# A Strassen form for the products of attention into the model, with the outputs normalized by a row from DRAM

## The chip, the cores and the metric

The kernel runs on one core of one Trainium2 chip. The metric is the device time of one execution in microseconds (us), the median of the runs shown. Five engines work side by side, each in the order of its own program: TensorE (PE) multiplies matrices, VectorE (DVE), ScalarE (ACT) and GpSimd (POOL) work on rows of 128 partitions, and SyncE (SP) issues transfers between DRAM and the memory on the chip. TensorE writes to PSUM, which has eight banks of 128 x 512 single-precision numbers, and the other engines read the result from there.

## The reference, cut to what matters

The sizes are S = 2048 rows, D = 576, 32 query heads on 16 key heads of width 128, the last W = 512 keys only, and a hidden width F = 4608, all in single precision.

```python
sa, ca, ga, sb, cb, gb = split(silu(c) @ w_mod)          # six rows of D
h = layernorm(x) * (1 + ca) + sa
q = (h @ wq) by heads;  k, v = caches[:, :, Sk - W:, :]  # two query heads per key head
o = softmax(q k^T / sqrt(128)) v
x = x + ga * (o @ wo)
h = layernorm(x) * (1 + cb) + sb
out = x + gb * ((silu(h @ w1) * (h @ w3)) @ w2)
```

The change is in `o @ wo`. Head by head this is a sum over 32 products of a [2048, 128] matrix with a [128, 576] one.

## The kernel before, in words

The rows are four blocks of 512. The first half of attention works on blocks 0 and 1, the second on blocks 2 and 3. A *slot* is one head on one block; `slots` lists 128 of them, 64 for each half, and slots 4k to 4k + 3 are two heads (2k' and 2k' + 1) on the two blocks. A slot is cut into four *steps* of 128 rows. A single-precision product is made from three fast ones: each operand is split into a high part, rounded to fp32r by a cast on ACT, and a low part, the difference, and high x high, high x low and low x high are added in PSUM. `split` (L82) does it: ACT casts, and DVE or POOL subtracts.

In iteration i of the main loop (at the end of the function) each step t transposes a quarter of the probabilities of slot i - 1 (`turn`), makes the scores of slot i, a quarter of the query of slot i + 1, and `attend_out(i - 2, t)`. After the fourth step `values(i - 1)` multiplies the probabilities into the values and leaves them in the PSUM tile `po`.

`values` (L344) splits `po` into a high and a low part, ACT casting and DVE subtracting, and takes the reciprocal r of the softmax's sums. `attend_out` (L361) calls `back` (L276), six matmuls 128x288 into the single PSUM tile E, of two banks, and DVE evicts E with one instruction, accumulator + r * E (L366). So the division by the softmax's sum is made when the product is evicted, row by row.

Everything that is not in those steps is listed by hand: `at(i, t, task)` puts a task behind step t of iteration i, and `run(i, t)` issues the tasks of a step in the order in which they were listed. All engines and SP's queue keep the program's order. Transfers wait in SP's queue for what they need, and the ones behind them wait too.

Such tasks are: the loads and splits of the query weights (`load_in`, `split_in`, POOL subtracting), of the output weights (`load_out`, a gate multiplication on POOL, `split_out`), of keys and values; and the making of the weights for the second part of the kernel, the gated MLP. That part multiplies pairs of blocks by Strassen's seven block products already. Its weights are prepared during attention: `load_raw` issues twelve transfers of a block of w1 and w3, `make_set` in seven steps makes seven sums, splits them (ACT casts, POOL subtracts) and stores each to DRAM (L499). `load_rows` loads two row blocks of w2, `make_rows` multiplies them by the gate and takes four differences on POOL in one step (its step -1), and then in seven steps splits and stores the seven operands (`keep`, L536). `load_oset` loads them back. There are 36 gate sets and 19 pairs of rows, so 55 items of seven steps.

In the second half the first two blocks, whose attention is complete, are also normalized and turned for the MLP (`norm`, `store_h`), and `combine` with `stage` makes the seven sums of h and stores them to DRAM: 21 steps on ACT, POOL and SP. `load_set` loads them. Buffers come from rings by tag: `hs` has 7 large buffers for h, raw weights and sets; `xn`, `w`, `hf`, `raw`, `o` are smaller ones.

Of the kernel before, what the change touches and what calls it, by code (L numbers as in the profile page):

```python
# [16 lines left out]
P = 128  # L17
# [21 lines left out]
def tile_block(  # L39
# [112 lines left out]

    norms = {}

    def norm_stats(b, t):
# [138 lines left out]
    n = len(slots)  # L294
    state = [dict() for _ in range(n)]
    hT, wqs, keys, vals, wos = {}, {}, {}, {}, {}
# [47 lines left out]
    def values(i):  # L344
        half, h, b = slots[i]
        st = state[i]
        vh, vl = vals[half, h // 2]
        pt = st["pt"]
        po = bank("A", "po")
        for j in range(KC):  # L350
            nc.tensor.matmul(po, vh[:, j, :], pt[0][:, j, :], start=j == 0, stop=False)  # L351
            nc.tensor.matmul(po, vl[:, j, :], pt[0][:, j, :], start=False, stop=False)  # L352
            nc.tensor.matmul(po, vh[:, j, :], pt[1][:, j, :], start=False, stop=j == KC - 1)  # L353
        oh = pool.tile([P, SB], F32R, tag="ah", name="oth", bufs=3)
        ol = pool.tile([P, SB], F32R, tag="al", name="otl", bufs=3)
        split(oh, ol, po, nc.vector)
        r = odd.tile([P, ST], F32, tag="r", name="r", bufs=3)
        nc.vector.reciprocal(r, st["l"])
        st["o"], st["r"] = (oh, ol), r

    def attend_out(i, t):  # L361
        half, h, b = slots[i]
        st = state[i]
        back(st["o"], wos[half, h], t)
        a = half_split(acc[b][:, t, :])
        nc.vector.scalar_tensor_tensor(a, E[:, :, :HALF], st["r"][:, t : t + 1], a, op0=ALU.mult, op1=ALU.add)  # L366
# [26 lines left out]
    def combine_tiles(pair):  # L393

        if pair == 0:
            a = pool.tile([P, DC + 1, SB], F32, tag="hs", name="hc", bufs=HB)
            return [a[:, k, :] for k in range(DC + 1)]
        tiles = [pool.tile([P, SB], F32, tag="xn", name="hc", bufs=ST) for _ in range(4)]
        return tiles + [pool.tile([P, SB], F32, tag="raw", name="hc", bufs=RB)]
# [33 lines left out]
    def combine(pair, c, step, tiles):  # L433
# [6 lines left out]
        elif step == 1:  # L440
            sub(h12, h12, h11)
            stage(pair, "p2", c, h21)
        elif step == 2:
            sub(h11, h22, h12)
            stage(pair, "p7", c, t3)
        elif step == 3:
            stage(pair, "p5", c, h12)
        elif step == 4:
            stage(pair, "p6", c, h11)
            sub(h21, h21, h11)  # L450
        elif step == 5:
            stage(pair, "p3", c, h22)
        else:
            stage(pair, "p4", c, h21)

    def load_set(pair, k):
# [5 lines left out]
    works = {}  # L462
    staged = [0]

    def staging(shape, name):

        staged[0] += 1
        tag, bufs = (("xn", ST), ("w", 8))[staged[0] % 2]
        return pool.tile(shape, F32R, tag=tag, name=name, bufs=bufs)
# [45 lines left out]
    odram[LAST, 4] = dram.tile([P, 2, 2, HALF], F32, name="od_plain")  # L515

    def chunks(d):

        return d if d < G else FLIP if d == G else d - G - 1

    def load_rows(p):

        whole = pool.tile([P, 7, HALF], F32, tag="hs", name="w2raw", bufs=HB)
        for j in range(2):
            f = NF - 1 - j if p == FLIP else 2 * p + j
            nc.sync.dma_start(whole[:, 2 * j : 2 * j + 2, :], half_split(w2[f * P : (f + 1) * P, :]))
        works["o", p] = whole
# [10 lines left out]
    def make_rows(p, n):  # L538
# [3 lines left out]
        if n < 0:  # L542
            for j in range(2):
                r = whole[:, 2 * j : 2 * j + 2, :]
                nc.gpsimd.tensor_mul(r, r, half_split(gates["b"]))
            nc.gpsimd.tensor_sub(t1, b12, b11)
# [48 lines left out]
    def finish(pair, t, eng):  # L595

        m15, m6 = msums[pair][0][t], msums[pair][1][t // 2][:, t % 2, :]
        a = half_split(acc[2 * pair + 1][:, t, :])
        eng.tensor_add(m6, m6, m15[:, 0, :])
# [3 lines left out]
        eng.tensor_add(m15[:, 1, :], m15[:, 1, :], m6)  # L603
        if pair == 0:
            store_out(1, t)

# [15 lines left out]
    def down(d, u):  # L622
# [23 lines left out]
        else:  # L646
            nc.vector.tensor_add(into, ps[:, :, :HALF], into)

    def multiply(ps, jobs):
# [128 lines left out]
    def gate(into, key, kind):  # L778
        nc.gpsimd.tensor_mul(into[key], into[key], gates[kind])

    first = {}
    for i, (half, h, b) in enumerate(slots):
        first.setdefault((half, h), i)
    for key, i in first.items():
        h, kv = key[1], (key[0], key[1] // 2)
        if i >= 2:
            at(i - 3, 1, load, wqs, key, load_in, wq, h * DH)
            at(i - 2, 1, put, wqs, key, split_in)
        at(*(i - 2, 1) if i > 2 else (0, -1), load, wos, key, load_out, wo, h * DH)
        at(*(i - 1, 0) if i > 2 else (1, 1), gate, wos, key, "a")  # L790
        at(max(i - 1, 1), 2, put, wos, key, split_out)
        if i and h % 2 == 0:
# [6 lines left out]
    last_group = len(groups) - 1  # L799
    early = [4 * i + t for lo, hi in ((10, 57), (66, 75)) for i in range(lo, hi) for t in range(ST)]  # L800
    late = [4 * i + t for i in range(85, 117) for t in range(ST)]
    items = []
    for p in range(G + 1):
        for f in (2 * p, 2 * p + 1) if p < G else ():
            items += [(load_raw, make_set, f, k) for k in range(7)]
        items += [(load_rows, make_rows, p, k) for k in range(7)]
    soon = len(early) * 5 // 4
    for number, (loader, maker, w, k) in enumerate(items):
        if number < soon:
            step = early[number * len(early) // soon]  # L810
        else:
            step = late[(number - soon) * len(late) // (len(items) - soon)]
        if k == 0:
            lead = 6 if maker is make_set else 11
            at((step - lead) // 4, (step - lead) % 4, loader, w)
            if maker is make_rows:
                at((step - 4) // 4, (step - 4) % 4, maker, w, -1)
        at(step // 4, step % 4, maker, w, k)
    for k, (i, t) in zip(ORDER, ((n - 4, 0), (n - 4, 1), (n - 4, 3), (n - 3, 0), (n - 3, 1), (n - 3, 2), (n - 2, 0))):
# [15 lines left out]
    for d in range(2 * G):  # L835
# [7 lines left out]
        for q, (i, t) in times:  # L843
            at(("m", i), t, load_oset, d, q)
    for pair, i in ((0, 2 * HQ + 23), (1, ("m", 14))):
        at(i, 0, split_x, pair)
# [23 lines left out]

    for i, b in ((52, 2), (2 * HQ + 6, 0)):
        for k in range(2):
# [19 lines left out]

    for b, i in ((0, 2 * HQ + 12), (1, 2 * HQ + 16)):
        norm(i, b)
        for m in range(DC + 1):
            at(i + 1 + m // 3, m % 3, store_h, b, m, "T", "hf")
    at(2 * HQ + 21, -1, begin_parts, 0)
# [94 lines left out]
    for i in range(n + 2):  # L992
        run(i, -1)
        for t in range(ST):
# [11 lines left out]
            if 2 <= i:  # L1006
                attend_out(i - 2, t)
            run(i, t)
# [32 lines left out]
```

## Time and profile before

| what | value |
| --- | --- |
| median of 3 runs | 3064.2 us (3063.02 to 3065.59) |
| the profiled execution, its own time | 3066.29 us |
| its span, first to last instruction | 3064.5 us |
| mean granted clock of TensorE | 0.996 |
| bytes moved by DMA | 523.13 MB, mean 171 GB/s |
| a slot in the second half | 13.9 us |

In the profile, PE is TensorE's matmuls and PEld its weight loads; L282 is line 282 of the kernel; `pe<-o,oth` names what an instruction writes and what it reads. Matmuls overlap, so the length of one record is longer than the time after which the next one starts. A row of the grouped view has the busy time, the mean of one in ns, and the idle time ahead of it with what ended it. A row of the timeline has the start, the length, the engine and the line.

### The profile page before, as it was taken

The numbers are of one execution on the slowest core, as the hardware profiler recorded it, in microseconds if no ns is written. First come the engines' busy times: TensorE is split into PE (matmuls) and PEld (weight loads), VectorE is DVE, ScalarE is ACT, GpSimd is POOL, SyncE is SP. The second block draws the span as 40 slices with busy tenths as digits, with TensorE's granted clock in tenths as the row PEclk, the third lists the DMA queues.
The fourth block names the chain that finished last, engine by engine and source line by source line (L and its number), as shares of the span: only waits on it lengthen the run. The fifth ranks groups of instructions, "written<-read, shape, count | busy, mean of one in ns | idle before, by whom it ended". The sixth has DMA issues, their size and how long they took to land.

```text
span 3064.5 us, 47936 instructions
## 1 busy us (share of the span) xinstructions
PE 3027.4 (99%) x16948; PEld 2654.4 (87%) x16948; DVE 2002.5 (65%) x3042; ACT 1481.7 (48%) x3107; POOL 1635.3 (53%) x1656
## 2 busy tenths in 40 slices
PE   7999999999999999999999999999999999999998
PEld 6888888888888888888888888888888888888887
DVE  6776676777777777777777766555555555555555
ACT  4556666666666665666665553333333222322222
POOL 3257887888734731667775103346555463443444
PEclk8999999999999999999999999999999999999999
DMA  4235546555512532354544135667666766666664
GB/s 143 76 130 191 184 163 198 182 184 184 179 42 76 181 101 65 127 183 168 160 163 149 40 141 187 210 219 259 240 229 219 279 238 193 203 200 203 199 197 141
DMA packets 330128, 523.13 MB, mean 171 GB/s; under 512 B 32800, under 2 KB 161824, under 8 KB 328096
## 3 DMA queue, kind: packets, MB, share of 16 engines
q1 hardware_dynamic: 329280, 520.06, 51.5%
q8 instruction: 135, 2.21, 0.3%
q14 instruction: 105, 0.86, 0.1%
q10 hardware_dynamic: 608, 0.00, 0.0%
HBM read 369.76 MB, written 150.18 MB: 170 GB/s over the span
## 4 chain that ended last, share of the span: by engine, by line
PE 94%; DVE 2%; POOL 2%; ACT 1%; issue 1%; DMA 1%; SPq 0%; ACTq 0%; POOLq 0%; DVEq 0%
PE py L577 15%; PE pe L282 13%; PE px L577 11%; PE pq L266 11%; PE pt L335 7%; PE pf L653 6%; PE pe L653 6%; PE po L353 4%; PE po L352 4%; PE po L351 4%; PE pss L317 4%; PE pss L315 4%; PE pss L316 4%; PE pq L274 2%; PE pt L252 0%
## 5 line engine op out<-in xcount | busy, mean ns | idle before, releaser
L325 ACT ACTIVATE p<-pss,nm 128x512 f32<-128x512 f32 x512 | 353.3, 690 | 367.4 <-DVE nm L319 367.1
L577 PE MATMUL py<-hset,wset 128*128 128x512 f32 x2016 | 506.9, 391 | 0.0
L366 DVE SCALAR_TENSOR_TENSOR acc<-pe,r,acc 128x576 f32<-128x576 f32 x512 | 416.8, 814 | 53.6 <-PE pe L282 47.9
L319 DVE TENSOR_REDUCE nm<-pss 128x1 f32<-128x512 f32 x512 | 349.7, 683 | 118.2 <-PE pss L317 118.0
L577 PEld LDWEIGHTS py<-hset,wset 128*128 128x128 f32 x2016 | 362.6, 188 | 58.9
L577 PE MATMUL px<-hset,wset 128*128 128x512 f32 x1512 | 380.1, 391 | 0.0
L282 PEld LDWEIGHTS pe<-o,oth 128*128 128x128 f32 x2048 | 326.7, 188 | 48.7 <-DVE acc L366 6.1
L342 DVE TENSOR_TENSOR ptl<-pt,pth 128x512 fp32r<-128x512 f32 x512 | 349.0, 682 | 16.1 <-ACT pth L336 15.6
L282 PE MATMUL pe<-o,oth 128*128 128x288 f32 x2048 | 355.8, 296 | 2.7 <-DVE acc L366 2.6
L336 ACT CAST pth<-pt 128x512 fp32r<-128x512 f32 x512 | 301.1, 588 | 37.1 <-PE pt L335 33.3
L577 PEld LDWEIGHTS px<-hset,wset 128*128 128x128 f32 x1512 | 275.6, 188 | 49.4
L335 PE MATMUL pt<-ident,p 128*128 128x128 f32 x2048 | 307.7, 273 | 4.6 <-DVE ptl L342 2.6
L85 POOL TENSOR_TENSOR akv<-u,akv 128x512 fp32r<-128x512 f32 x141 | 182.1, 1302 | 237.8 <-ACT akv L84 236.3
L335 PEld LDWEIGHTS pt<-ident,p 128*128 128x128 f32 x2048 | 249.8, 141 | 18.6 <-issue 3.0
L315 PE MATMUL pss<-kh,qh 128*128 128x512 f32 x512 | 244.9, 478 | 0.7 <-ACT qh L84 0.7
L85 DVE TENSOR_TENSOR otl<-po,oth 128x512 fp32r<-128x512 f32 x128 | 88.6, 692 | 225.8 <-ACT oth L84 225.8
L497 POOL TENSOR_TENSOR wmade<-wraw,wmade 128x256 fp32r<-128x256 f32 x252 | 186.6, 740 | 80.5 <-ACT wmade L496 62.0
L282 PE MATMUL pe<-o,otl 128*128 128x288 f32 x1024 | 219.0, 295 | 0.0
L84 ACT CAST oth<-po 128x512 fp32r<-128x512 f32 x128 | 75.1, 587 | 295.6 <-PE po L353 295.6
L317 PE MATMUL pss<-kh,ql 128*128 128x512 f32 x512 | 202.9, 396 | 0.0
L316 PE MATMUL pss<-kl,qh 128*128 128x512 f32 x512 | 202.6, 396 | 0.0
L353 PE MATMUL po<-ptl,vh 128*128 128x512 f32 x512 | 201.1, 393 | 1.2 <-DVE ptl L342 1.2
(181 smaller groups left out, 6522.7 us busy)
## 6 DMA issues: line engine op xcount, KB each, us to landing
oset<-od SPq DMA_DIRECT2D x106, 576.0 KB, 4.8
od<-omade SPq DMA_DIRECT2D x133, 288.0 KB, 2.7
oraw<-in_A_wo SPq DMA_DIRECT2D x64, 288.0 KB, 3.1
wraw<-in_B_w SPq DMA_DIRECT2D x144, 128.0 KB, 2.7
wraw<-in_A_wq SPq DMA_DIRECT2D x64, 256.0 KB, 3.2
w2raw<-in_B_w SPq DMA_DIRECT2D x38, 288.0 KB, 3.6
oset<-od SPq DMA_DIRECT2D x35, 288.0 KB, 3.3
wraw<-in_B_w SPq DMA_DIRECT2D x288, 32.0 KB, 2.1
```

The source lines that it names most:

```text
L266: nc.tensor.matmul(ps, (wh if k < 2 else wl)[:, m, :], hT[DC + m if k == 1 else m], start=s == 0, stop=False,)
L282: nc.tensor.matmul(E[:, h, :HALF], a[:, rows], b[:, h * HALF : (h + 1) * HALF], start=n == 0, stop=n == 2)
L315: nc.tensor.matmul(pss, st["qh"][:, rows], kh, start=True, stop=False)
L316: nc.tensor.matmul(pss, st["qh"][:, rows], kl, start=False, stop=False)
L317: nc.tensor.matmul(pss, st["ql"][:, rows], kh, start=False, stop=True)
L319: nc.vector.tensor_reduce(nm, pss, axis=AX.X, op=ALU.max, negate=True)
L325: nc.scalar.activation(p, pss, AF.Exp, bias=nm, accum_out=st["l"][:, t : t + 1])
L335: nc.tensor.transpose(ps[:, j, :], p[:, j * P : (j + 1) * P], ident)
L342: nc.vector.tensor_sub(pt[1][:, :, cols], state[i]["t"], pt[0][:, :, cols].bitcast(F32))
L366: nc.vector.scalar_tensor_tensor(a, E[:, :, :HALF], st["r"][:, t : t + 1], a, op0=ALU.mult, op1=ALU.add)
L577: nc.tensor.matmul(ps, w[:, a, :], h[:, b, :], start=start and n == 0, stop=stop and n == 6, skip_group_check=True)
L653: nc.tensor.matmul(ps[:, h, :HALF], a[:, rows], w[:, b, :], start=m == 0, stop=m == 2)
```

## The change

For heads 4 to 27 of the second half (slots 72 to 119, twelve groups of two heads on two blocks, `FAST`), the products into the model are made as seven block products. With X the 2 x 2 blocks of outputs (two blocks of rows, two heads) and B the 2 x 2 blocks of the output weights (two heads, two halves of D), Winograd's form of Strassen's method needs seven products of sums of X and of B in place of eight. A group has 84 matmuls 128x288 in place of 96.

The sums need outputs that are already divided by the softmax's sums, and in `po` the rows of the model lie along the free dimension. So `invert` writes the reciprocals of a slot to DRAM, transposed, and `spread` reads them back as one row over all 128 partitions; `values` multiplies `po` by it. The weights of these heads are made like those of w2, as twelve more pairs of rows among the items, loaded with `load_oset`. `out_sum` makes the sums of X on POOL, `out_split` splits the seven operands (two with POOL, five with DVE), and `out_unit` makes 14 units of six matmuls into E, each with one addition on DVE. They run from the third step of the fifth slot after a group's first slot on, one unit in a step, with two steps left out in each sixteen.

The partial sums lie where the accumulators of blocks 0 and 1 were: these are stored to DRAM ahead and loaded back after attention, and the subtraction that readies block 1 for the MLP moves to the MLP's second group. Block 3's accumulator is kept as a difference while the new form runs, so heads 28 and 29 use weights that are also split as a difference (`put_turned`); `finish_out` and `finish_out_first` add the sums up. The items' steps are spread anew: 33 of them in slots 10 to 56 as before, and the other 22 with the twelve new ones in slots 66 to 116 (before, the rest lay in slots 66 to 74 and 85 to 116). The statistics, the normalization and the combining of blocks 0 and 1 move ahead, and the combining is made in 15 slots where it had 24.

```diff
+    FAST = range(18, 30)
 def values(i):
...
+        if i // 4 in FAST:
+            nc.vector.tensor_mul(blocks[i], po, sums_home[3])
+            return
...
+    def invert(i):
+        r = odd.tile([P, ST], F32, tag="r", name="r", bufs=3)
+        nc.vector.reciprocal(r, state[i]["l"])
+        state[i]["row"] = dram.tile([ST, P], F32, name=f"r{i}")
+        nc.sync.dma_start(state[i]["row"].rearrange("t p -> p t"), r)
+
+    def spread(i):
+        row = state[i].pop("row").rearrange("t p -> (t p)")
+        nc.sync.dma_start(sums_home[3], row.partition_broadcast(P))
...
+    PAIRS_OF_HEADS = [("a", k - 16) for k in FAST]
...
+            w, f = (wo, 2 * p[1] + j) if type(p) is tuple else (w2, NF - 1 - j if p == FLIP else 2 * p + j)
...
+    def out_unit(k, u):
+        b, d = slots[4 * k][0], ("a", k - 16)
+        m15, m6 = sums_home[:2]
+        if u < 4:
+            q, into, jobs = 0, half_split(acc[b + 1][:, u, :]), [("p4", 0, u), ("p7", 1, u)]
...
+        multiply(E, [(halves[d, name], osets[d, q][:, i], r) for name, i, r in jobs])
+        if k == FAST[0] and q in (1, 2):
+            nc.vector.tensor_copy(into, E[:, :, :HALF])
+        else:
+            nc.vector.tensor_add(into, E[:, :, :HALF], into)
+
+    def out_sum(k, what):
+        x00, x01, x10, x11 = (blocks[4 * k + i] for i in range(4))
+        if what == "s3":
+            nc.gpsimd.tensor_sub(sums_home[2], x00, x01)
+        elif what == "s1":
+            nc.gpsimd.tensor_add(x01, x01, x11)
+        elif what == "s2":
+            nc.gpsimd.tensor_sub(x11, x01, x00)
+        else:
+            nc.gpsimd.tensor_sub(x10, x10, x11)
+
+    def out_split(k, name):
...
+        hi, lo = [pool.tile([P, SB], F32R, tag=t, name=f"o{t}", bufs=3) for t in ("ah", "al")]
+        split(hi, lo, x, nc.gpsimd if name in ("p7", "p2") else nc.vector)
+        halves[("a", k - 16), name] = hi, lo
...
+    EARLY = 33
+    late, places = made[EARLY:], []
+    for j, p in enumerate(PAIRS_OF_HEADS):
+        lo, hi = (len(late) * k // len(PAIRS_OF_HEADS) for k in (j, j + 1))
+        places += [(load_rows, make_rows, p), *late[lo:hi]]
+    for these, lo, hi in ((made[:EARLY], 10, 57), (places, 66, 117)):
+        for number, (loader, maker, w) in enumerate(these):
+            for k in range(7):
+                step = 4 * lo + (7 * number + k) * 4 * (hi - lo) // (7 * len(these))
+                if k == 0:
+                    lead = 6 if maker is make_set else 7
+                    at((step - lead) // 4, (step - lead) % 4, loader, w)
+                    if maker is make_rows:
+                        at((step - 4) // 4, (step - 4) % 4, maker, w, -1)
+                at(step // 4, step % 4, maker, w, k)
...
-        i = 2 * HQ + 22 + 8 * c
+        i = 2 * HQ + 18 + 5 * c
         at(i, -1, fill_parts, 0, c)
         for step in range(7):
-            at(i + 1 + step, 1, combine_parts, 0, c, step)
+            at(i + 1 + step // 2, 1 + 2 * (step % 2), combine_parts, 0, c, step)
...
+    for k in FAST:
+        s, d = 4 * k, ("a", k - 16)
+        for i in range(s, s + 4):
+            at(i + 1, 0, invert, i)
+            at(i + 1, 2, spread, i)
+        for what, i, t in (("s3", 3, 1), ("s1", 5, 0), ("s2", 5, 2), ("s4", 7, 2)):
+            at(s + i, t, out_sum, k, what)
+        for name, i, t in (("p7", 4, 1), ("p4", 5, 0), ("p6", 5, 3), ("p1", 6, 1), ("p5", 6, 2), ("p2", 7, 1), ("p3", 8, 0)):
+            at(s + i, t, out_split, k, name)
+        for q, (i, t) in enumerate(((4, 3), (5, 2), (6, 0), (7, 0))):
+            at(s + i, t, load_oset, d, q)
+        for u in range(14):
+            step = 4 * (s + 5) + 2 + u + (u >= 10)
+            at(step // 4, step % 4 + 0.5, out_unit, k, u)
...
-                attend_out(i - 2, t)
+                if (i - 2) // 4 not in FAST:
+                    attend_out(i - 2, t)
+            run(i, t + 0.5)
             run(i, t)
```

More of the change, by code (lines that the diff above doesn't have):

```diff
@@ L363, in attend_out @@
         st = state[i]
-        back(st["o"], wos[half, h], t)
+        back(st["o"], wos.get((half, h, b)) or wos[half, h], t)
         a = half_split(acc[b][:, t, :])
@@ L844, in tile_block @@
             at(("m", i), t, load_oset, d, q)
-    for pair, i in ((0, 2 * HQ + 23), (1, ("m", 14))):
+    for pair, i in ((0, ("m", 1)), (1, ("m", 14))):
         at(i, 0, split_x, pair)
```

116 lines of the change are left out of this document (78 added, 38 removed).

## The prediction, made before the changed kernel was run

> **What bounds the kernel now.** I read the page first: busy shares, then the chain that ended last.
>
> ```profile
> PE 3027.4 (99%) x16948; PEld 2654.4 (87%) x16948; DVE 2002.5 (65%) x3042; ACT 1481.7 (48%) x3107; POOL 1635.3 (53%) x1656
> ...
> PE 94%; DVE 2%; POOL 2%; ACT 1%; issue 1%; DMA 1%; SPq 0%; ACTq 0%; POOLq 0%; DVEq 0%
> ```
>
> TensorE sets the end: 94% of the chain. A matmul taken away is a gain only while DVE, ScalarE, GpSimd (POOL) and SyncE's queue (SP) keep up. So the second view is busy time by stretch (window, length, then PE, PEld, DVE, ACT, POOL, and last clock, DMA share, GB/s):
>
> ```profile
> 0.00:100.00 100.00, 81.20 (x411) 66.78 (x412) 70.67 (x119) 49.95 (x96) 34.29 (x36) 0.90 0.42 129
> 300.00:700.00 400.00, 399.18 (x2278) 349.58 (x2277) 283.76 (x440) 259.12 (x592) 321.05 (x390) 1.00 0.56 183
> 1000.00:1300.00 300.00, 299.41 (x1726) 262.94 (x1725) 218.42 (x362) 179.70 (x396) 148.36 (x165) 1.00 0.37 120
> 1300.00:1500.00 200.00, 200.00 (x1145) 175.76 (x1144) 141.19 (x220) 126.08 (x286) 143.39 (x158) 1.00 0.53 176
> ```
>
> PE is full in both halves of attention, even where POOL is 80% busy (300 to 700). In the second half POOL has only 49 to 72%.
>
> Third, the time of one slot (one head on one block), from the first and last of the 30 reciprocals between two answers on L358: (1849.5 - 1431.9)/30 = 13.92 us.
>
> ```profile
> L358 DVE RECIPROCAL r<-l x98: 166/168/170, 64.3 to 1431.9; 128x4 f32<-128x4 f32 x98
> L358 DVE RECIPROCAL r<-l x128: 166/168/170, 64.3 to 1849.5; 128x4 f32<-128x4 f32 x128
> ```
>
> Fourth, the order of time inside one slot (start, length, engine):
>
> ```profile
> 500.41 0.70 PE L282 MATMUL pe<-o,oth 128*128 128x288 f32 x4
> 500.94 0.43 PE L282 MATMUL pe<-o,otl 128*128 128x288 f32 x2
> 501.21 0.60 PE L335 MATMUL pt<-ident,p 128*128 128x128 f32 x4
> 501.42 0.82 DVE L366 SCALAR_TENSOR_TENSOR acc<-pe,r,acc 128x576 f32<-128x576 f32 x1 [0.21 <-PE pe L282]
> ...
> 506.80 0.40 PE L353 MATMUL po<-ptl,vh 128*128 128x512 f32 x1
> 507.04 0.60 PE L335 MATMUL pt<-ident,p 128*128 128x128 f32 x4
> ...
> 509.39 0.43 PE L282 MATMUL pe<-o,otl 128*128 128x288 f32 x2
> 509.65 0.60 PE L335 MATMUL pt<-ident,p 128*128 128x128 f32 x4
> ...
> 511.48 0.69 PE L282 MATMUL pe<-o,oth 128*128 128x288 f32 x4
> ```
>
> A step (a quarter of a slot) is 507.04 to 509.65, 2.61 us; the last has more query products and the values behind it. The products into the model are issued every (500.94 - 500.41)/4 = 0.133 us. That pitch, not the 0.3 us of a single record, is what one of them is worth.
>
> **The products.** Four slots (two heads, two blocks) took 4 x 24 = 96 such matmuls; seven block products take 7 x 12 = 84. Twelve groups: 144 fewer, 144 x 0.133 = **-19.1 us**.
>
> **The end of the new stretch.** Units are issued five slots behind their group, the plain product two. So in slots 122 to 125 twelve steps hold both, back to back in the one PSUM tile E. The second waits for the first's eviction: L366 above ends at 502.24 where the next matmul began at 501.21, 1.03 us. Twelve times: **+12.4 us**. (The 14 steps without E at the start are in the 19.1 already.)
>
> **DVE and ScalarE.** Per group DVE loses 16 evictions of 0.814 and gains 14 additions of 0.752 and five splits from SBUF at 1.153; the multiplication by the row has the size of the subtraction it replaces (0.692).
>
> ```profile
> L366 DVE SCALAR_TENSOR_TENSOR acc<-pe,r,acc 128x576 f32<-128x576 f32 x512 | 416.8, 814 | 53.6 <-PE pe L282 47.9
> L647 DVE TENSOR_TENSOR acc<-pe,acc 128x576 f32<-128x576 f32 x140 | 105.3, 752 | 53.9 <-PE pe L653 52.8
> L85 DVE TENSOR_TENSOR otl<-po,oth 128x512 fp32r<-128x512 f32 x128 | 88.6, 692 | 225.8 <-ACT oth L84 225.8
> L85 DVE TENSOR_TENSOR aal<-u,aah 128x512 fp32r<-128x512 f32 x37 | 42.7, 1153 | 26.0 <-ACT aah L84 26.0
> ```
>
> That is -13.0 + 10.5 + 5.8 = +3.3 us, 0.8 per slot on 218/300 = 73% of 13.9, so 11 of 13.5 us: counted at nothing behind TensorE (without that cover 48 x 0.8 = 38 us). ScalarE is at 60 to 63% and stays below. The moved accumulators, the later subtraction for the first pair and the smaller pool of staging tiles I put at nothing: other heads' products hide them.
>
> **The row, which is the term that decides.** It must pass through SP. At the slot's first step the reciprocal is written to DRAM, at its third the row is read back over all partitions, and DVE's multiplication behind the values waits for it. Queued behind that wait are DVE's next maximum, low part and eviction of E; PE's next unit waits for the latter. How late may the row be? From the third step's end (501.21) to the end of the values (507.20) are 6.0 us. If the multiplication starts there, 0.69 + 0.69 + 0.68 + 0.75 us later E is free, at 510.0, and PE wants it at 511.48: with hand-overs some 1.2 us more. So the row must land 7.2 us after the third step. A 256 KB load lands in 3.1 us, 3.2 with the fuller queue, so SP may come to it **4.0 us** late.
>
> ```profile
> oset<-od SPq DMA_DIRECT2D x106, 576.0 KB, 4.8
> ...
> kvraw<-in_A_v_cache SPq DMA_DIRECT2D x32, 256.0 KB, 3.1
> hd0p<-hst SPq DMA_DIRECT2D x35, 256.0 KB, 2.3
> ```
>
> (Fuller, because a group adds four loads of products' weights, 2.0 MB, seven stores of 288 KB and four rows of 256 KB: 5 MB in 54 us, 93 GB/s on the 120 to 176 of the windows. At 4.8 us, as the larger loads take, each late row would cost 1.6 more.)
>
> The write is 512 elements of 4 bytes; the nearest is the load of c by single elements (4.0/4.3/4.6 us, the last line below), 4.3.
>
> ```profile
> 1400.29 0.98 SPq L478 DMA_DIRECT2D wraw<-in_B_w  x2
> ...
> 1404.30 1.88 SPq L481 DMA_DIRECT2D wraw<-in_B_w  x4
> ...
> 1430.36 10.44 SPq L499 DMA_DIRECT2D wd31p<-wmade  x2
> ...
> DMA to landing us min/median/max: 4.0/4.3/4.6
> ```
>
> SP goes in program order. The first two rows are the first and the last of the twelve issues of one gate set's load: 5.9 us. The third shows SP held 10.4 us by stores whose POOL work was late; nobody needed soon what lay behind them. Why POOL was late:
>
> ```profile
> 1421.27 0.46 POOL L498 TENSOR_TENSOR wmade<-wraw,wmade 64x128 fp32r<-64x128 f32 x1
> 1422.95 1.57 POOL L85 TENSOR_TENSOR wl<-wraw,wh 128x640 fp32r<-128x640 f32 x1 [1.23 <-ACT wh L84]
> ...
> 1430.41 2.83 POOL L545 TENSOR_TENSOR w2raw<-w2raw,gate_b 128x576 f32<-128x576 f32 x2
> 1433.20 0.81 POOL L546 TENSOR_TENSOR w2raw<-w2raw 128x288 f32<-128x288 f32 x1
> ...
> 1437.91 1.30 POOL L85 TENSOR_TENSOR vl<-kvraw,vh 128x512 fp32r<-128x512 f32 x1
> ...
> 1419.61 0.81 DVE L366 SCALAR_TENSOR_TENSOR acc<-pe,r,acc 128x576 f32<-128x576 f32 x1
> 1433.26 0.82 DVE L366 SCALAR_TENSOR_TENSOR acc<-pe,r,acc 128x576 f32<-128x576 f32 x1
> ```
>
> The gate and four differences of one pair of rows are 2.83 + 4 x 0.81 = 6.1 us in one step. The two DVE rows mark the ends of first steps: POOL finished those steps' work 2.1 (1421.73) and 5.9 us (1439.21) late. So b, the lag with which SP reaches a step, is 2.1 to 5.9; I take 3, nearer the lower, which had no burst ahead of it.
>
> The new list puts 34 items in slots 66 to 117, item n beginning at step 264 + 6n. Loads of gate sets stand at 258 + 6n, bursts of rows at 260 + 6n: always a first or third step, where the row's two issues stand behind them. From slot 73 there are twelve set loads. Eight stand in third steps, where the read is 5.9 + b - 4.0 = 1.9 + b too late; four in first steps, where write and landing (5.9 + 0.4 + 4.3 = 10.6) overrun the two steps between (5.2) by 5.4, so 1.4 + b. With b = 3: 8 x 4.9 + 4 x 4.4 = **57 us**. Six bursts stand in first steps: POOL has 6.1 and two steps' makes (some 3.3) to do within 5.2, so 0.2 + b: **19 us**. In third steps a burst comes behind the read and is mostly drained: nothing.
>
> ```profile
> L497 POOL TENSOR_TENSOR wmade<-wraw,wmade 128x256 fp32r<-128x256 f32 x252 | 186.6, 740 | 80.5 <-ACT wmade L496 62.0 <-issue 7.1 <-POOL wmade L498 4.2
> L498 POOL TENSOR_TENSOR wmade<-wraw,wmade 64x128 fp32r<-64x128 f32 x252 | 116.2, 461 | 19.8
> L533 POOL TENSOR_TENSOR omade<-w2raw,omade 128x288 fp32r<-128x288 f32 x134 | 106.8, 810 | 79.9 <-ACT omade L532 65.3 <-DMA wraw<-in_B_w 6.6 <-DMA hc<-h 5.2
> L693 POOL TENSOR_TENSOR s<-u,u 128x512 f32<-128x512 f32 x35 | 45.3, 1294 | 65.0 <-DVE u L750 65.0
> L490 POOL TENSOR_TENSOR wraw<-wraw 128x384 f32<-128x384 f32 x36 | 36.6, 1017 | 1.0
> ```
>
> In slots 82 to 97 the combining of h is now pressed into 15 slots. An item is 7 x 1.20 + 4 x 1.02 = 12.5 us (set) or 2 x 1.42 + 11 x 0.81 = 11.8 (rows); 10.7 of them are 130 us. Four groups' sums and splits are 24 x 1.29 = 31, query weights and values 8 x 1.57 + 4 x 1.30 = 18, combining 12 x 1.29 + 28 x 1.3 = 52. POOL: 231 us. PE: 16 x (13.92 - 0.40) = 216. POOL overflows by 15 us and never gets its lag down: between 15 us more and 5.9 (the larger b) in each of the 12 slots that combine, 71. I take **40**, about the middle, since no row is nearer to either.
>
> The sum: -19.1 + 12.4 + 57 + 19 + 40 = **+109 us** on the profiled execution's 3066.3 (span 3064.5), which is 2.1 above the median: 3175 there, **3174** as a median. With b = 2.1 and 15 for the combining it is +68, with landings of 2.3 instead of 3.2 us at 31 late rows another -28: 3104. With b = 5.9 and 71: +192, 3256.
>
> The Trainium skill's page "DMA: Bandwidth & Descriptors", section "Anatomy of one DMA", gives a fixed 2.0 us plus bytes/436 GB/s: 2.6 us for the row and 2.0 for the write. By that estimate the third-step delays shrink by 0.6 us each, and the sum by some 20 us. The loads of this trace took 3.1, so the sum keeps the rows.
>
> **Rivals.** *The row comes in time*: SP's lag costs nothing, as it does now, because the loads run ahead in the pauses that POOL still has (it is 80% busy at 300 to 700 with PE full). Then -19.1 + 12.4 = -7, 3057, and 3045 if the double steps hide too. For it: DVE no longer waits 1.8 us per slot for ScalarE (225.8/128). Against it: the 10.4 us row. It turns where SP's lag at the third step stays under 4.0 us.
>
> *Only POOL's work counts*: it overflows in slots 82 to 97 but each row comes early enough: -7 + 15 = +8, 3072. Against it: the row is needed in the slot in which it is made.
>
> *The clock falls too.* In the first 100 us PE idled 18.8 and was granted 0.90, so 10 us lost for 18.8 idle, 0.53 per us. The 116 us of stalls would cost 62 more: 3236. The Trainium skill's "TensorE: Matmul & The Clock Gate", Part 1, says that an idle window brings the clock back to half; that row agrees, though start-up may be the reason, and no row shows it for a stall.
>
> **How the numbers follow.** Likeliest 0.60; row in time 0.22; only POOL 0.10; clock 0.08. The likeliest's own range is 3104 to 3256. Both signs hold weight, so the range goes to 3055, which takes in half of the first rival, and ends at 3240. A change under about 0.2% (6 us) can't be told from none. Faster takes 0.14 from the first rival, the rest of it, 0.08, is no change; slower 0.78.
>
> **What would show it.** DVE's multiplication in slots 72 to 119 idle behind a DMA of the row, over 1 us, most in slots 82 to 98; PE under 95% there; SP's store of a made set holding the row's issues; idle PE in slots 122 to 125 behind L366, about 1 us each. If DVE waits for TensorE instead and PE stays at 99%, the row's term is wrong; if POOL's lag stays under 4 us in slots 82 to 97, so is the 40.

## The result

The changed kernel takes **3497.9 us** (median of 4 runs, 3496.8 to 3500.9) against 3064.9: a ratio of 1.142, 95% interval 1.140 to 1.143. It is slower, as forecast, but by 433 us where 109 were forecast, and outside the range.

The page of the changed kernel: busy shares, the clock by slices, and the chain that ended last.

```profile
PE 3119.4 (89%) x16804; PEld 2703.7 (77%) x16804; DVE 2024.4 (58%) x3082; ACT 1511.9 (43%) x3205; POOL 1830.2 (52%) x1861
...
PEclk9999999999998888787887889999999999999999
...
PE 40%; DMA 15%; DVE 4%; POOL 4%; issue 4%; ACT 2%; SPq 1%; DVEq 0%; POOLq 0%; ACTq 0%
PE py L603 13%; PE px L603 9%; DMA r<-r 7%; PE pe L718 7%; PE pf L718 6%; DMA acc<-r 5%; PE pt L339 1%; DMA wraw<-in_A_wq 1%; PE pq L267 1%; DVE nm L323 1%; DVE os L360 1%; PE pe L283 1%; POOL omade L559 1%; DVE oal L85 1%; SPq L500 0%
```

TensorE's share of the chain falls from 94 to 40%. Two transfers stand in it, the reciprocals' write (`r<-r`) and the row's read (`acc<-r`). By stretch (columns as in the prediction):

```profile
300.00:700.00 400.00, 397.97 (x2271) 348.67 (x2270) 282.05 (x437) 256.88 (x587) 316.11 (x383) 1.00 0.55 181
1100.00:1500.00 400.00, 270.56 (x1310) 225.61 (x1310) 171.02 (x272) 163.67 (x375) 229.28 (x251) 0.83 0.65 152
1500.00:2100.00 600.00, 419.46 (x2028) 354.63 (x2027) 273.40 (x432) 237.75 (x549) 302.46 (x321) 0.84 0.63 139
```

The first half is untouched. In the new stretch TensorE is busy 68 to 70% at a clock of 0.83 to 0.84, and nothing else is full: neither DVE (43 to 46%) nor POOL (50 to 57%). Something is waited for in turn. The instructions on L360 (the multiplication by the row), their idle time, and the landings of the two transfers, first the write and then the read:

```profile
L360 DVE TENSOR_TENSOR os<-po,acc x48: 691/692/693, 1092.5 to 2138.1; 128x512 f32<-128x512 f32 x48
...
  DMA acc<-r: 370.2, 46
...
DMA to landing us min/median/max: 9.2/9.5/11.0
...
DMA to landing us min/median/max: 5.3/5.6/6.1
```

Of 48 multiplications 46 waited for the row, 370 us together, and 47 intervals took 1045.6 us: **22.2 us a slot** where it was 13.9. The chain of waits over two slots, in order of time:

```profile
1506.96 0.69 DVE os L360
1507.65 0.61 DVE nm L323
...
1512.21 9.58 DMA r<-r
1521.79 0.02 issue
1521.81 5.62 DMA acc<-r
...
1527.55 0.69 DVE os L360
1528.24 0.61 DVE nm L323
...
1530.86 1.31 DVE oal L85
1532.16 0.10 DVE r L374
1532.26 0.02 issue
1532.28 11.00 DMA r<-r
1543.28 0.02 issue
1543.30 6.07 DMA acc<-r
```

A reader should see a ring here: write, read, multiplication, a few DVE and POOL instructions, the next slot's reciprocal, the next write. Averaged over the slots, by the starts in the timeline, a turn is 11.7 us from the issue of the write to that of the read, 4.9 from there to the multiplication, 3.3 to the next reciprocal and 2.5 to the next write; the last part, and what the first has over the landing of 9.5, is mostly SP coming late. The whole loss lies in attention: its last reciprocal, at 1849.5 us before, now comes at

```profile
L368 DVE RECIPROCAL r<-l x80: 166/168/172, 63.3 to 2281.4; 128x4 f32<-128x4 f32 x80
```

which is 432 us later, and from there to the end of the span are 1215 us in both.

### The profile page after: what moved, and what is told of

Read it like the earlier page. It is cut to its first block, busy times and chain, and to the rows that moved or that the text cites. A ratio compares the mean times of both kernels' runs of the same rounds, so it can differ in the third digit from the quotient of the medians.

```text
span 3496.4 us, 48599 instructions
## 1 busy us (share of the span) xinstructions
PE 3119.4 (89%) x16804; PEld 2703.7 (77%) x16804; DVE 2024.4 (58%) x3082; ACT 1511.9 (43%) x3205; POOL 1830.2 (52%) x1861
## 4 chain that ended last, share of the span: by engine, by line
PE 40%; DMA 15%; DVE 4%; POOL 4%; issue 4%; ACT 2%; SPq 1%; DVEq 0%; POOLq 0%; ACTq 0%
PE py L603 13%; PE px L603 9%; DMA r<-r 7%; PE pe L718 7%; PE pf L718 6%; DMA acc<-r 5%; PE pt L339 1%; DMA wraw<-in_A_wq 1%; PE pq L267 1%; DVE nm L323 1%; DVE os L360 1%; PE pe L283 1%; POOL omade L559 1%; DVE oal L85 1%; SPq L500 0%
## 5 line engine op out<-in xcount | busy, mean ns | idle before, releaser
L339 PE MATMUL pt<-ident,p 128*128 128x128 f32 x2048 | 329.6, 286 | 169.6 <-DVE kl L257 73.5
L339 PEld LDWEIGHTS pt<-ident,p 128*128 128x128 f32 x2048 | 263.0, 148 | 195.5 <-issue 98.3
L559 POOL TENSOR_TENSOR omade<-w2raw,omade 128x288 fp32r<-128x288 f32 x218 | 175.7, 817 | 264.6 <-ACT omade L558 248.9
L718 PE MATMUL pe<-oset,oah 128*128 128x288 f32 x672 | 160.3, 329 | 150.5 <-ACT oah L84 85.9
L388 DVE SCALAR_TENSOR_TENSOR acc<-pe,r,acc 128x576 f32<-128x576 f32 x320 | 260.4, 814 | 33.3 <-PE pe L283 29.5
L718 PEld LDWEIGHTS pe<-oset,oah 128*128 128x128 f32 x672 | 130.4, 214 | 177.6 <-ACT oah L84 88.5
L319 PE MATMUL pss<-kh,qh 128*128 128x512 f32 x512 | 257.4, 503 | 0.7 <-ACT qh L84 0.7
L360 DVE TENSOR_TENSOR os<-po,acc 128x512 f32<-128x512 f32 x48 | 33.2, 692 | 384.3 <-DMA acc<-r 370.2
L283 PEld LDWEIGHTS pe<-o,oth 128*128 128x128 f32 x1216 | 194.1, 188 | 31.1 <-DVE acc L388 6.1
L283 PE MATMUL pe<-o,oth 128*128 128x288 f32 x1216 | 212.1, 296 | 2.4 <-DVE acc L388 2.2
```

Source lines behind the costliest of these rows:

```text
L283: nc.tensor.matmul(E[:, h, :HALF], a[:, rows], b[:, h * HALF : (h + 1) * HALF], start=n == 0, stop=n == 2)
L319: nc.tensor.matmul(pss, st["qh"][:, rows], kh, start=True, stop=False)
L339: nc.tensor.transpose(ps[:, j, :], p[:, j * P : (j + 1) * P], ident)
L718: nc.tensor.matmul(ps[:, h, :HALF], a[:, rows], w[:, b, :], start=m == 0, stop=m == 2)
```

## The experiments

Times are of single runs beside a kernel before of 3064 to 3068, with four runs where an interval is given; the four of `const_row` lie between 3192 and 3198, so a few microseconds between single runs say nothing. Line numbers are those of each kernel.

| run | time, us | from one multiplication to the next, us |
| --- | --- | --- |
| the change | 3498 | 22.2 |
| `early`: write listed earlier | 3436 | 20.7 |
| `no_items_row`: no later items, row as changed | 3370 | 19.7 |
| `runs16`: write in runs of 16 bytes | 3349 | 19.1 |
| `no_write`: read only | 3327 | 18.7 |
| `no_items_early`: no later items, write earlier | 3238 | 16.8 |
| `pitch8`: row of ones, slow combining | 3200 | 16.1 |
| `row_on_act`: row through ScalarE's queue | 3198 | 16.1 |
| `const_row`: row of ones | 3197 | 16.0 |
| `relief`: that, early weights, slow combining, three sums on DVE, exact | 3193 | 16.0 |
| `fewer_issues`: row of ones, loads in 6 pieces | 3193 | 15.9 |
| `best1`: row through ScalarE's queue, early weights, sums on DVE, exact | 3189 | 15.7 |
| `oset_early`: row of ones, early weights | 3175 | 15.6 |
| `xdve`: row of ones, early weights, sums on DVE | 3172 | 15.4 |
| `no_items`: row of ones, no later items | 3094 | 13.9 |
| `no_items_order`: the same, other order in double steps | 3088 | 13.9 |

**How much is the row?** A row of ones takes both transfers away.

```diff
+        nc.gpsimd.memset(sums_home[3], 1.0)
...
-            at(i + 1, 0, invert, i)
-            at(i + 1, 2, spread, i)
```

> The changed kernel without both transfers of the row: DVE multiplies the outputs of heads 4 to 27 by a row of ones that stays in place, so these heads are not divided by their softmax sums; all else is the change. Theory A (the two landings of the row, 9.5 and 5.6 us one behind the other, are nearly the whole loss): DVE's multiplication waits for the values alone and the time falls to 3058 to 3080 us. Theory B (POOL's overflow in slots 82 to 97 and SP's lag hold TensorE by themselves): 3100 us or more, with PE under 95% in those slots. The product term of the prediction (-19.1 + 12.4) would show as 3057 if nothing else is lost.

Measured: 3196.7 us, ratio 1.043 (1.041 to 1.045). That is theory B's range, but both theories hold a part: the row costs 301 us, and 132 stay without it. TensorE's waits in the new stretch of this run:

```profile
PE pe L718 <- DMA oset<-ad: 41.9, 8, 11.9
PE pt L339 <- DVE kl L257: 12.7, 4, 5.5
PE pe L718 <- DVE acc L388: 10.6, 9, 1.8
```

The longest is for the loads of the products' weights, which stand in SP's queue as the row did. The sum of the prediction did not have them.

**Read, write, or order?** Three runs change one thing each.

```diff
# no_write: no reciprocal, every read is of one fixed row of ones
-        nc.sync.dma_start(sums_home[3], row.partition_broadcast(P))
+        nc.sync.dma_start(sums_home[3], sums_home[4].partition_broadcast(P))
...
-            at(i + 1, 0, invert, i)
...
# runs16; the multiplication then reads the row at a stride of four
...
-        state[i]["row"] = dram.tile([ST, P], F32, name=f"r{i}")
-        nc.sync.dma_start(state[i]["row"].rearrange("t p -> p t"), r)
+        state[i]["row"] = dram.tile([P, ST], F32, name=f"r{i}")
+        nc.sync.dma_start(state[i]["row"], r)
...
# early
-            at(i + 1, 0, invert, i)
+            at(i, 3, invert, i)
```

> The row is read from DRAM for every slot as in the change, but from one fixed row of ones; no reciprocal is taken and none written (heads 4 to 27 are not divided by their softmax sums). Theory A: without the write's 9.5 us the read of 5.6 us still lands 5.6 us after SP comes to it, against 7.2 allowed, so SP may be 1.6 us late: I expect 60 to 160 us of loss to stay (3120 to 3220 us). Theory C (the write is what costs, the read is hidden): under 3090 us. Theory B: hardly below 3400.

> The same result by another layout in DRAM: each partition writes its four reciprocals as one run of 16 bytes, 128 runs in place of 512 single elements; the row then holds them in the order row, step, and DVE reads it with a stride of four. Nothing else is changed. If the 9.5 us are the number of pieces, the write lands in 3.5 to 5 us, each slot is some 5 us shorter where DVE waited, and the time is 3200 to 3300 us. If they are the distance to DRAM, the write stays over 8 us and the time within 40 us of 3498.

> The write of single elements is kept, but reciprocal and write are listed behind the last step of the slot itself, ahead of the multiplication of the slot before, and no longer behind the first step of the next; the read stays where it was. Theory A: the write begins about 5.4 us earlier and no longer waits for the multiplication before it, so an undisturbed slot has its row 1 to 2 us before it is late, and what stays is SP's lag: 3150 to 3280 us. Theory B (SP's and POOL's lag is the whole loss): 3420 to 3500 us, since the same work is queued ahead of the read.

Measured: 3327.5, 3348.7 and 3435.6 us, all three above theory A's ranges (by 107, 49 and 156 us), the last in theory B's. The ranges left out the 132 us that stay without any row. Counted from the row of ones, the read alone costs 131 us: it landed in 4.1 us, and DVE still waited 210 us for it, because SP came late. Its stores waited 261 us for POOL's `omade` and 171 for `wmade` in that stretch, and in one slot the read stood behind twelve issues of set loads, from 1501.0 to 1508.0 us: this is the lag that the prediction described. In runs of 16 bytes the write landed in 3.5 us (median) where it took 9.5, and 149 us went. `early` bought only 62: the write was listed earlier but landed in 11.0 us, and SP's lag stayed (16.9 us on average from the issue of the write to that of the read). By `no_write` the write is the larger half of the row's cost, 170 of 301 us, and lag in the queue matters with it. The landings, `runs16` write and read, then `early` write and read:

```profile
DMA to landing us min/median/max: 1.4/3.5/6.6
...
DMA to landing us min/median/max: 3.5/4.2/6.4
```

```profile
DMA to landing us min/median/max: 9.8/11.0/13.9
...
DMA to landing us min/median/max: 3.5/4.7/12.9
```

**Can the row be had for nothing?** Both remedies, and ScalarE's queue for the two transfers:

```diff
+        nc.scalar.dma_start(state[i]["row"], r)
...
+        nc.scalar.dma_start(sums_home[3], row.partition_broadcast(P))
...
+            at(i, 3, invert, i)
+            at(i + 1, 1, spread, i)
```

> The same result with the row made independent of SP: the reciprocal is taken behind the slot's last step, written in runs of 16 bytes, and both transfers are issued from ScalarE's queue, the read behind the second step of the next slot. What stays is the change without a late row. If the loss is the sum of two separate terms (the late row, about 305 us, and POOL's lag, about 126 us, which the kernel with a row of ones still showed), DVE's wait for the row is under 30 us in total and the time is 3180 to 3230 us. If the row's own landing still binds (write and read over 13 us together), the wait stays over 100 us and the time over 3260.

Measured: 3198.5 us, as with the row of ones. DVE's multiplication no longer waited for a transfer; its instructions and what ended their idle time:

```profile
L361 DVE TENSOR_TENSOR os<-po,acc x48: 1024/1084/1126, 1080.2 to 1839.1; 128x512 f32<-128x512 f32 x48
its engine sat idle before it (us, times) until:
  PE po L357: 35.5, 38
```

So the three edits together take away the row's 300 us, and what is left is another thing.

**What are the other 130 us?** First three guesses: two single edits, both with a row of ones, and a bundle with the exact row.

```diff
# oset_early
-        for q, (i, t) in enumerate(((4, 3), (5, 2), (6, 0), (7, 0))):
+        for q, (i, t) in enumerate(((3, 0), (4, 0), (5, 1), (6, 2))):
# pitch8
-        i = 2 * HQ + 18 + 5 * c
+        i = 2 * HQ + 18 + 8 * c
...
-            at(i + 1 + step // 2, 1 + 2 * (step % 2), combine_parts, 0, c, step)
+            at(i + 1 + step, 1, combine_parts, 0, c, step)
# relief: row_on_act, both edits above, and s1, s2 and s4
-            nc.gpsimd.tensor_sub(x11, x01, x00)
+            nc.vector.tensor_sub(x11, x01, x00)
```

> A row of ones in place (heads 4 to 27 are not divided by their softmax sums), and the four loads of a group's weights are listed 7 to 11 steps ahead of their use in place of 3 to 5, as early as the ring of three buffers allows. Nothing else. With the row of ones TensorE waited 41.9 us for these loads (8 times, up to 11.9 us). Theory B1 (POOL's lag reaches TensorE through SP and these loads): that wait falls under 10 us and the time from 3190 to 3130 to 3155 us. Theory B2 (the lag reaches it through ScalarE and the sums as much): the wait falls, but the time stays over 3170, since the next late thing takes its place.

> A row of ones in place (heads 4 to 27 are not divided by their softmax sums), and the combining of h takes 24 slots again, one step in a slot, as before the change, in place of 15. POOL's work is the same but no longer 231 us in 16 slots. By the stage term of the prediction (15 to 71 us) the time falls from 3190 by about as much, to 3120 to 3175 us; if the combining is not the place, it stays within 12 us of 3190.

> The same result with all of it: the row through ScalarE's queue as above, the weights' loads early, the combining over 24 slots, and three of the four sums of a group (s1, s2, s4) on DVE in place of POOL. If late rows and POOL's backlog are the whole loss, TensorE is full again (over 98% in slots 74 to 121) and the time is 3052 to 3080 us: 3064 less 19 for the products, 12 more for the double steps, up to 20 for what is left. If something else stalls TensorE (DVE's load, the clock by itself, the buffers), it is over 3110.

Measured: 3174.9, 3200.3 and 3192.9 us (`relief` 1.041, 1.039 to 1.044). Early weights took their 42 us of waits away and gave 22 us: theory B2, the next late thing took the place. The first two waits of that run were 12.7 and 4.1 us in `const_row`:

```profile
PE pt L339 <- DVE kl L257: 26.1, 6, 7.4
PE pe L718 <- DVE acc L693: 17.8, 4, 6.6
PE pe L718 <- DVE acc L388: 14.1, 12, 1.8
```

The pressed combining is not the place: spread out, with a row of ones, it cost the same. And `relief` missed its range by 113 us. In it DVE stood 30.5 us, eight times, for POOL's split of p2, ahead of s4, which I had moved to DVE.

**Is it the items?** Then the 22 later items were left out, with a row of ones and with the row as changed; in a third run POOL lost all sums and splits of X, and a fourth is that one with the exact row.

```diff
# no_items, no_items_row: the MLP reads the first 22 gate sets and 8 pairs in place of the later ones
-        places += [(load_rows, make_rows, p), *late[lo:hi]]
+        places += [(load_rows, make_rows, p)] + [None] * (hi - lo)
...
# xdve, best1: also s1 to s4, and the early loads of oset_early
-        split(hi, lo, x, nc.gpsimd if name in ("p7", "p2") else nc.vector)
+        split(hi, lo, x, nc.vector)
```

> A row of ones in place (heads 4 to 27 are not divided by their softmax sums), and the 22 later items (14 gate sets, 8 pairs of rows of w2) are not made in slots 66 to 117: the MLP reads the first 22 gate sets and 8 pairs in their place, so half of its weights are others. The twelve pairs of heads keep their places. POOL has some 264 us less to do in these slots and SP 14 loads of 5.9 us less to issue. Theory B (POOL's and SP's backlog is what the row of ones left, 126 us): TensorE is over 97% in slots 74 to 121 and the time 3050 to 3080 us. Theory D (the sums and splits of X themselves, on DVE and ScalarE, stall it): 3130 us or more.

> As in the run before, the 22 later items are not made, but the row goes through DRAM as in the change, divided by the softmax sums. It has no late loads of sets and hardly any burst ahead of it, so it shows the row's two landings by themselves: with 9.5 and 5.6 us a slot is late by 4.1 us without any lag, or, where the multiplication before it holds the reciprocal, a cycle of some 20 us per slot in place of 13.5. Theory A1 (the cycle closes in every slot): 3300 to 3400 us. Theory A2 (4 us each): 3230 to 3290. If the landings matter only through SP's lag: under 3150.

> A row of ones in place (heads 4 to 27 are not divided by their softmax sums), the weights' loads early, and all sums of X and the two splits that POOL made on DVE, so that nothing in the products' path but their weights comes from POOL. All items are made. POOL has 7.8 us per group less, DVE about as much more. Theory B: POOL's lag no longer touches the products, and the time falls to 3065 to 3110 us. Theory D: DVE is then too full (12.6 of 13.5 us in a slot) and it stays over 3150.

> The same result as before the change: the row in runs of 16 bytes through ScalarE's queue, the weights' loads early, all sums and splits of X on DVE. It adds to the last one the row's two issues on ScalarE and a multiplication of 1.07 in place of 0.69 us. If the terms add up, it is 10 to 25 us over the run with the row of ones: 3075 to 3135 us; it beats the kernel before only if that one is under 3050.

Measured: 3093.9, 3369.7, 3172.5 and 3189.3 us. Without the items 103 of the 132 us are gone, so they are the larger part, though 3094 is 14 us above the range. The row by itself, without these items, is 276 us: theory A1, a ring of 19.7 us. (The twelve pairs of heads and the combining still stand in the queues there, but SP comes to the write only 0.7 us after the reciprocal on average, where it was 2.5.) Its multiplications by the row:

```profile
L360 DVE TENSOR_TENSOR os<-po,acc x48: 678/691/694, 1086.9 to 2010.7; 128x512 f32<-128x512 f32 x48
...
  DMA acc<-r: 305.5, 45
```

Moving the sums to DVE gave 2.5 us beyond the early weights, no more than single runs differ. That is theory D's range, but its reason isn't seen: DVE was busy 72% of 1000 to 2000 us. `best1` is 17 us over `xdve`, as its terms should add, but 54 us above its range, since `xdve` was not where the sum had it. From 1100 to 1800 us, first without the items (`no_items`), then with them (`const_row`):

```profile
1100.00:1800.00 700.00, 670.60 (x3734) 575.34 (x3732) 501.42 (x740) 385.63 (x860) 317.26 (x279) 1.00 0.35 114
```

```profile
1100.00:1800.00 700.00, 612.24 (x3264) 518.98 (x3264) 438.72 (x646) 390.11 (x897) 528.00 (x565) 0.94 0.56 189
```

TensorE is at 96% without them and at 87% with them, with POOL at 45 and 75%.

**The last three questions:** does the ring close; do the items act through SP's issues; are the double steps dear?

```diff
# no_items_early: no_items_row, and
-            at(i + 1, 0, invert, i)
+            at(i, 3, invert, i)
...
# fewer_issues: const_row, and for later sets two transfers in place of eight
+                nc.sync.dma_start(whole[:, 2 * i : 2 * i + 2, 2, :], w[: 2 * P, cols].rearrange("(c p) n -> p c n", p=P))
+                continue
...
# no_items_order: no_items, and ahead of the query's products
+            if i >= 4 * FAST[-1] + 6:
+                run(i, t + 0.5)
```

> Without the 22 later items (the MLP reads earlier weights in their place), row through DRAM in single elements as in the change, but reciprocal and write listed behind the slot's own last step, ahead of the multiplication of the slot before. The landings stay near 10 and 5.5 us; only the order changes, so no reciprocal waits behind a late multiplication. Theory A1 (write, read, multiplication and next reciprocal close a cycle of 19.7 us per slot, which is what made 3370 of 3094): the cycle is open, most rows land in time, and the time is 3100 to 3190 us. If the landings load the path in another way (traffic, the queue), it stays over 3280.

> A row of ones in place, and all 22 later items are made, but each of the 14 later gate sets is loaded with 6 transfers in place of 12 (the last 64 rows of w1 and w3 are taken from other rows, so the later MLP weights are wrong; heads 4 to 27 are not divided by their softmax sums). POOL's work is unchanged, SP issues 2.9 us less per set. If the items' 96 us (3190 against 3094) come from SP's issuing, the time falls by 25 to 50 us from 3190; if from POOL's work, by less than 12.

> As the run with a row of ones and without the 22 later items (3094 us; heads 4 to 27 not divided by their softmax sums, half of the MLP's weights others), but in the twelve double steps of slots 122 to 125 the unit stands ahead of the query's products, so that its eviction runs beside 0.7 us or more of them. If the double steps cost 12 to 14 us as the term of the sum says, TensorE's waits for L388 fall by half or more and the time by 6 to 11 us, to 3083 to 3089. If the steps' cost is elsewhere, it stays within 3 us of 3094.

Measured: 3237.9, 3192.5 and 3087.9 us. The order alone takes 132 of the ring's 276 us, though the landings did not shrink (10.5 and 5.3). The edit both takes the reciprocal out from behind the late multiplication and starts the write earlier; the run doesn't tell the two apart. Its multiplications:

```profile
L360 DVE TENSOR_TENSOR os<-po,acc x48: 653/692/694, 1087.3 to 1877.3; 128x512 f32<-128x512 f32 x48
...
  DMA acc<-r: 147.0, 29
```

That is less than expected, 48 us above the range: 29 rows still came late, 147 us together. The two landings alone, 15.8 us, are longer than a slot of 13.9, and from the issue of the write to that of the read were 12.5 us on average; what SP's order adds wasn't tried. The number of SP's issues is not how the items act: half of them for each set gave 4 us, and the four runs of `const_row` differ by 6. What is left of the items is POOL's work with ScalarE's casts, the stores and the bytes that are moved, which these runs don't tell apart. The other order gave 6.1 us, which is what was forecast, but the kernel before was also 3.5 us faster beside that run (3064.3) than beside `no_items` (3067.8), so the time alone doesn't settle it. TensorE's twelve waits in the double steps, before it:

```profile
PE pe L725 <- DVE acc L388: 14.0, 12, 1.8
```

They are 14.0 us in `no_items` and absent with the other order, which waited 6.6 us for the unit's own eviction: 7.4 us less by the waits.

## Why the prediction was right or wrong

**The direction and the place were right, the mechanism in part.** The row through DRAM decided, DVE waited for it, and SP's queue carried other work's lag to it. The prediction named the wait that fills the trace after, but it had only some rows late, by SP's lag, where 46 of 48 were late.

**The step that failed is the row's own latency.** The prediction said the write lands in 4.3 us, by the load of c in single elements, and the row in 3.2, by loads of 256 KB. They measured 9.5 and 5.6: 15.1 in place of 7.5. The write was priced by a load made in the first microseconds of the program, but it is a store, made amid all the other transfers; which of the two made the difference wasn't tried. In 128 pieces of 16 bytes, in place of 512 of 4, the store landed in 3.5 us in the same place, so the layout is most of it (the number of the pieces and their size changed together). By the prediction's own allowance this makes every slot late without any lag: from the end of the first step the two landings are 15.1 us, before the reciprocal and the issues are added, against 5.2 + 7.2 = 12.4.

**The second fault is in the form of the sum.** It added delays slot by slot, as if each write began on time. A late multiplication delays the next reciprocal, which the program puts behind it, and so the next write: a ring of 9.5 + 5.6 + 4 to 5 = 20 us that runs for itself. `no_items_row` shows it at 19.7 us without the 22 items, and `no_items_early` at 16.8 with the reciprocal ahead of the late multiplication. In the changed kernel the turn is 22.2: the items' lag comes on top of the ring, 128 us (3498 against 3370).

**The terms for late rows** (57 for the set loads, 19 for the bursts) were priced as what SP and POOL add to an otherwise timely row. In the changed kernel that case did not exist; where it did, with the read alone (`no_write`), 35 rows were late and the loss was 131 us. Fewer issues for the set loads were worth at most 4 us once the row was gone (`fewer_issues`); with the row they were not tried apart.

**The 40 us for the combining** were put in the wrong place. The items do cost, but not there: `pitch8` changed nothing, and the 22 items in all of slots 66 to 117 cost 103 us with a row of ones. (A slip beside it: the lower bound counts 31 late rows, where its terms have 8 + 4 + 6 + 12 = 30; it is worth 0.9 us.)

**The rival "only POOL's work counts"** gave +8; its run is `const_row`, +132. It counted the overflow of POOL's work in 16 slots and left out other things for which TensorE then waits: the products' weights (41.9 us in `const_row`), the keys (12.7) and ScalarE's casts (7.2). How the lag reaches TensorE isn't settled: taking one way out gave 22 us, and with more taken out 3172 to 3193 stayed.

**The rival "the row comes in time"** fell: 46 of 48 came late. Its price would have been wrong too: a row in time gave 3197, not 3057.

**The rival "the clock falls too"** came true beside the likeliest. The clock was 0.83 to 0.84 in the new stretch, 0.94 with the row of ones, and 1.00 over the same stretch of `no_items`, where TensorE was 96% busy. The Trainium skill's "TensorE: Matmul & The Clock Gate", Part 1, has the half clock return after an idle window; these rows agree with it. TensorE was busy 92 us longer than before (3119.4 against 3027.4 us) with 144 matmuls fewer. How much of that is the clock, and how much matmuls that stood alone and no longer overlapped, no run shows, since no run has the stalls without the clock.

**The products' 19.1 us** were never seen as a gain. In `no_items` a slot of its fullest stretch takes (1690.7 - 1402.8)/21 = 13.71 us, 0.21 under 13.92 where 0.40 were forecast:

```profile
L360 DVE TENSOR_TENSOR os<-po,acc x22: 690/692/693, 1402.8 to 1690.7; 128x512 f32<-128x512 f32 x22
```

```profile
1400.00:1700.00 300.00, 295.95 (x1664) 255.97 (x1664) 223.44 (x328) 164.56 (x372) 114.58 (x103) 1.00 0.34 111
```

TensorE was idle 4.05 us of these 300, which is 0.19 us a slot, so by this estimate a full slot has the 0.40 that was forecast. Waits elsewhere took back more than that: over all 48 slots one takes 13.94 us. The unit's matmuls keep the pitch of 0.13 us. **The double steps**, 12.4 us in the sum, measured 14.0 as waits.

The Trainium skill's estimate of 2.0 us for the write and 2.6 for the row ("DMA: Bandwidth & Descriptors", "Anatomy of one DMA") was further off than the rows: 9.5 and 5.6 decide. That section of the Trainium skill is on transfers that GpSimd issues; these were issued by SP. The same page of the Trainium skill, under "Rules for kernel authors", says that a last dimension that isn't contiguous becomes one descriptor per element and should be rearranged; `runs16` agrees, 9.5 to 3.5 us.

No version here beats the kernel before. The best exact one, `best1`, is 122 us above the kernel before beside it (3067.8), and even without the row and the later items the new form stands at 3088, 24 above.

## What to carry to other kernels

Before a value is sent through DRAM within a loop, write down the ring it closes: the landing of the store, the landing of the load, and every instruction that the program puts between the result and the next store; if the ring is longer than the loop's turn, no idle engine helps. Price a store by a store of the same piece size, since here 512 pieces of 4 bytes landed in 9.5 us and 128 of 16 bytes in 3.5, and list the producer ahead of the late consumer. With a row of ones TensorE fell to 87% though the fullest other engine, POOL, was busy 75% on average: queues that wait in order pass a lag on, so a change that fills the pauses of another engine has to be charged for its lag at every place that waits for it, not for its overflow.

## What the runs showed that I had not expected

The row's read landed in 4.7 to 5.6 us (medians) behind stores of single elements (`early` and the change) and in 4.1 to 4.6 without them (`no_write`, `runs16`, `row_on_act`), for the same 256 KB; why wasn't tried. The multiplication with a row read at a stride of four elements took 1.05 to 1.08 us where the contiguous one took 0.69. And taking 42 us of waits from TensorE bought 22.
